# Infini-attention block on one core: q and k projected from raw weights in 32-column tiles, heads regrouped, new orders

## The chip, the cores and the metric

One core of a Trainium2 chip runs the whole program. The metric is the device time of one execution in microseconds (us). The engines are TensorE (PE, with its weight loads shown apart as PEld), VectorE (DVE), ScalarE (ACT), GpSimd (POOL) and SyncE (SP), whose queue issues the transfers between HBM and the on-chip memory and the transposes by DMA.

## The reference

A pre-norm transformer block on one sequence of 2048 tokens, width 640, in bfloat16. Cut to what matters:

```python
x = A_x                                     # (1, 2048, 640)
h = x + A(layernorm(x))                     # attention with memory
h2 = h + silu(layernorm(h) @ w1) @ w2       # F = 1728

def A(x):                                   # H = 32 heads of Dh = 20, N = 4 segments of L = 512
    q, k, v = x @ wq, x @ wk, x @ wv        # split into heads and segments
    for s in range(4):
        p = softmax(qs @ ks.T * Dh**-0.5 + causal_mask)     # within the segment
        a_dot = p @ vs
        a_mem = (phi(qs) @ M) / (phi(qs) @ z + 1e-6)        # phi(t) = t+1 if t>0 else exp(t)
        out[s] = g * a_mem + (1 - g) * a_dot                # g = sigmoid(beta), per head
        M += phi(ks).T @ vs;  z += sum(phi(ks))
    return concat(out) @ wo
```

## The kernel before, in words

**Segments and stages.** The four segments of 512 tokens are worked off in one long list of small tasks. For each segment: layer norm of four blocks of 128 tokens (`n1_st` statistics, `n1_rs` the inverse deviation on POOL, `n1_ap` applied on DVE), a transpose (segment 0: on PE, `n1_tp`, brought back by `n1_te`; later: by DMA, `n1_tr`), the projections of q, k (`pr`, brought from PSUM to SBUF by `qe`) and v (`v`, `ve`), then eight ticks of four heads each. A tick has scores (`qk`), their exponentials on ACT (`e`, line 964 for two heads, 960 for four at once), the causal mask on POOL (`mk`), the product with v (`av`), scaling (`oe`), a transpose back (`td`), from segment 1 on the memory's part (`tm`), normalization (`nm`) and the sum of both (`ad`). `ex`, `pa`, `pb` make phi of k (of q too from segment 1 on); `kt`, `mz`, `ma`, `mb` update the memory. Behind come the output projection (`ot`, `wo`, `rs`), the second layer norm and the two matrix products of the dense part (`h1` with `th` and `s`, `h2` with `o`).

**Names of projection tasks.** `pr021.0` is segment 0, chunk 2 of five, k (0 is q), first three of the five blocks of the contraction; `.1` the other two. A chunk is 128 columns, four heads in four groups of 32 rows, of which a head takes 20. Scores read 20 rows at offsets 0, 32, 64 and 96, each as a tile of its own.

**What stands in the other 12 rows.** Five chunks hold 20 heads in their first 20 rows of each 32. The other 12 heads are packed into the 12 free rows of each 32: the first 12 of a head's 20 dimensions in chunks 0 to 2, the remaining 8 in chunks 3 and 4. Ticks 0 to 4 of a segment read the chunks directly; ticks 5 to 7 read the tile `QKV`, which 12 transfers per segment (`vt`, SP's queue) put together from the chunks. For this packing the columns of wq and wk are copied from the raw weights (in the tile `wraw`, on the place of `sT`) into `wqr` and `wkr` by `re_` tasks on DVE, ACT and POOL (lines 711 and 713) before they are used.

**Order.** Nothing is decided on the chip. A table `ORDER` names every task in the order in which it is emitted, with its engine (`/A`, `/D`, `/G`; `/C` is a PE task done as four tiles of 32 columns, `/W` the exponential of four heads at once) and its buffers. `Tracker` puts in the semaphore waits that the data and buffers need. Each engine works off its own part of the list in order. `fill` tasks are matmuls on zeros at the start.

**PE's three shapes.** A matmul on the whole 128x128 array (line 550), four matmuls of 32 columns side by side (lines 551, 999, 1117), and four matmuls of 20 contraction rows at four row offsets (line 943, the scores).

Of the kernel before, what the change touches and what calls it, by code (L numbers as in the profile page):

```python
# [5 lines left out]
ACT = mybir.ActivationFunctionType  # L6
# [228 lines left out]
class Graph:  # L235
# [52 lines left out]
    def schedule(self):  # L288
# [3 lines left out]
        for row in ORDER:  # L292
# [56 lines left out]
MZB = [0, 2, 4, 6, 9]  # L349
MZN = [2, 2, 2, 3, 3]  # L350

GRP_BLK = [[(0, 0)], [(1, 2)], [(2, 4)], [(3, 6)], [(4, 9)],
           [(0, 1), (3, 7)], [(1, 3), (4, 10)], [(2, 5), (3, 8), (4, 11)]]
# [3 lines left out]
SPLIT0 = ((0, 0), (0, 1))  # L357
# [112 lines left out]
def build(nc, es, A_x, A_wq, A_wk, A_wv, A_wo, A_beta, B_x, B_w1, B_w2, out):  # L470
# [76 lines left out]
    def mms(eng, out, lhsT, rhs, start, stop):  # L547

        if eng != "cols":
            return [lambda e: e.matmul(out, lhsT=lhsT, rhs=rhs, start=start, stop=stop)]  # L550
# [24 lines left out]
    for a in X:  # L575
        a.users += 1
# [329 lines left out]
    def declare_ticks(s):  # L906
# [421 lines left out]
```

## Time and profile before

| what | value |
|---|---|
| runs | 296.78 us median of 3 (296.61 to 297.32) |
| the profiled execution | 297.21 us, its span 295.2 us, clock 1.0 |
| busy: PE, DVE, ACT, POOL | 280.6, 219.0, 216.5, 148.2 us |
| the chain that ended last | PE 64%, ACT 17%, DVE 10%, issue 3% |

The span runs from the first to the last instruction of the profiled execution; 2.0 us of the execution's time lie outside it. The profiled execution is 0.43 us above the median. The chain that ended last is followed back from the last instruction, at each step to what released it; from about 52 us on it is mostly PE, ahead of that mostly ACT.

### The profile page before, as it was taken

What the parts mean: (1) busy time and instruction counts of PE and PEld (TensorE: products, weight loads), DVE (VectorE), ACT (ScalarE), POOL (GpSimd) and SP (SyncE); (2) the same over time, 40 slices, a digit from 0 to 9 for tenths busy, and PEclk for the clock granted to TensorE, in tenths of its full rate; (3) what the DMA queues carried; (4) which work ended last, traced back from release to release, by engine and by line L of the source; (5) the groups of instructions that cost most, each with busy time, mean ns of one, the idle gap of its engine ahead of it and who ended that gap; (6) DMA issues with size and microseconds to landing.
All of it is one profiled execution on the core that took longest, in us unless ns stands there. A gap on an engine that the chain in (4) does not pass through costs nothing.

```text
span 295.2 us, 8471 instructions
## 1 busy us (share of the span) xinstructions
PE 280.6 (95%) x3537; PEld 158.1 (54%) x3561; DVE 219.0 (74%) x447; ACT 216.5 (73%) x263; POOL 148.2 (50%) x297
## 2 busy tenths in 40 slices
PE   7899889899999999999999999999999999999996
PEld 5554434536644545566643564556564657764574
DVE  4788899689999677999879867597655676734614
ACT  5799999799989999957899856979989641004500
POOL 4878777662777436946527552548464621300000
PEclk9999999999999999999999999999999999999999
DMA  7859349476530400442553312303221031330003
GB/s 223 288 151 232 57 115 229 96 235 90 87 66 18 104 4 3 75 100 46 81 135 101 77 27 53 58 2 54 62 69 47 2 67 26 67 91 0 0 2 111
DMA packets 48597, 24.72 MB, mean 84 GB/s; under 512 B 38896, under 2 KB 47472, under 8 KB 48560
## 3 DMA queue, kind: packets, MB, share of 16 engines
q1 hardware_dynamic: 48560, 24.19, 34.9%
q8 instruction: 28, 0.46, 0.6%
q14 instruction: 9, 0.07, 0.1%
HBM read 10.41 MB, written 2.62 MB: 44 GB/s over the span
## 4 chain that ended last, share of the span: by engine, by line
PE 64%; ACT 17%; DVE 10%; issue 3%; DMA 2%; POOL 2%; ACTq 0%; DVEq 0%
PE ps_all L550 47%; ACT PT L964 12%; PE ps_all L551 7%; PE ps_all L943 5%; PE ps_all L999 4%; DVE stt L754 3%; ACT PT L960 2%; DVE xn_rot L772 2%; DVE sT L1222 2%; DMA tT<-otok 2%; ACT th L1216 1%; ACT ex L873 1%; POOL PT L976 1%; DVE x_tok L1181 1%; PE ps_all L1117 1%
## 5 line engine op out<-in xcount | busy, mean ns | idle before, releaser
L964 ACT ACTIVATE PT<-ps_all 128x1024 bf16<-128x1024 f32 x114 | 109.3, 1035 | 15.5 <-PE ps_all L943 14.8
L976 POOL TENSOR_SCALAR_AFFINE_SELECT PT<-PT 128x512 bf16<-128x512 bf16 x128 | 82.0, 649 | 57.5 <-ACT PT L964 32.0
L1216 ACT ACTIVATE th<-ps_all 128x512 f32<-128x512 f32 (+1 forms) x56 | 31.5, 585 | 36.6 <-PE ps_all L550 27.8
L550 PE MATMUL ps_all<-w_sb,sT 128*128 128x320 bf16 x400 | 58.2, 299 | 0.1
L550 PE MATMUL ps_all<-tT,w_sb 128*128 128x512 bf16 x225 | 53.9, 379 | 1.3 <-issue 1.1
L1222 DVE SCALAR_TENSOR_TENSOR sT<-th,ps_all 128x512 bf16<-128x512 f32 (+1 forms) x56 | 36.2, 663 | 17.7 <-ACT th L1216 17.1
L550 PEld LDWEIGHTS ps_all<-w_sb,sT 128*128 128x128 bf16 x400 | 38.1, 98 | 16.6 <-issue 1.5
L960 ACT ACTIVATE PT<-ps_all 128x2048 bf16<-128x2048 f32 x23 | 43.2, 1879 | 3.4 <-PE ps_all L943 3.0
L550 PEld LDWEIGHTS ps_all<-tT,w_sb 128*128 128x128 bf16 x235 | 21.4, 98 | 25.0 <-issue 1.8
L754 DVE BATCH_NORM_STATS2 stt<-x_tok 128x6 f32<-128x320 bf16 x62 | 26.8, 473 | 1.3 <-DMA x_tok<-in_A_x_dram 1.2
L1259 DVE SCALAR_TENSOR_TENSOR x_tok<-ps_all,x_tok 128x640 bf16<-128x640 f32 (+1 forms) x17 | 13.2, 784 | 18.0 <-PE ps_all L550 17.1
L1077 POOL TENSOR_TENSOR otok<-on 128x320 bf16<-128x320 bf16 x24 | 19.2, 806 | 12.5 <-DVE on L1069 12.5
L867 DVE CAST QK<-ps_all 128x512 bf16<-128x512 f32 x26 | 17.9, 687 | 8.0 <-PE ps_all L550 6.5
L764 POOL TENSOR_TENSOR rst<-mvt,eps_c 128x1 f32<-128x1 f32 x32 | 7.0, 219 | 31.9 <-DVE mvt L757 30.0
L550 PE MATMUL ps_all<-tT,wkr 128*128 128x512 bf16 (+1 forms) x87 | 21.7, 368 | 1.0 <-issue 0.5
L772 DVE TENSOR_SCALAR xn_rot<-x_tok,mvt,rst 128x640 bf16<-128x640 bf16 x32 | 17.8, 564 | 4.3 <-POOL rst L766 3.8
L550 PE MATMUL ps_all<-tT,wqr 128*128 128x512 bf16 (+1 forms) x79 | 20.0, 367 | 1.0 <-issue 0.6
L1069 DVE TENSOR_TENSOR on<-ps_all,rd 128x640 bf16<-128x640 f32 x24 | 19.8, 824 | 0.8
L550 PE MATMUL ps_all<-wv_sb,tT 128*128 128x320 bf16 x130 | 19.7, 299 | 0.7 <-issue 0.7
L766 POOL TENSOR_TENSOR rst<-rst,eps_c 128x1 f32<-128x1 f32 x32 | 18.0, 563 | 2.5
L1015 DVE TENSOR_SCALAR oTs<-ps_all,lsc 128x512 bf16<-128x512 f32 x24 | 17.8, 742 | 0.8 <-PE ps_all L999 0.8
L999 PE MATMUL ps_all<-PT,Vx 128*32 128x512 bf16 (+3 forms) x384 | 17.3, 301 | 0.0
(113 smaller groups left out, 379.5 us busy)
## 6 DMA issues: line engine op xcount, KB each, us to landing
out_dram<-x_tok SPq DMA_DIRECT2D x15, 160.0 KB, 1.9
w_sb<-in_B_w_dram SPq DMA_DIRECT2D x5, 432.0 KB, 4.7
x_tok<-in_A_x_dram SPq DMA_DIRECT2D x3, 640.0 KB, 4.3
w_sb<-in_B_w_dram SPq DMA_DIRECT2D x3, 480.0 KB, 4.1
QKV<-QK SPq DMA_DIRECT2D x12, 72.0 KB
wv_sb<-in_A_wv_dram SPq DMA_DIRECT2D x1, 800.0 KB, 8.0
wo_sb<-in_A_wo_dram SPq DMA_DIRECT2D x1, 800.0 KB, 4.9
w_sb<-in_B_w_dram SPq DMA_DIRECT2D x1, 640.0 KB, 5.1
```

Of the source, the lines that this page charges most:

```text
L550: return [lambda e: e.matmul(out, lhsT=lhsT, rhs=rhs, start=start, stop=stop)]
L551: return [lambda e, p=p: e.matmul(out[p:p + 32, :], lhsT=lhsT[:, p:p + 32], rhs=rhs, start=start, stop=stop, tile_position=(0, p)) for p i ...
L754: T.add(DV, lambda e, hh=hh: e.bn_stats(out=stt[:, s, 6 * hh:6 * hh + 6], in_=xb[:, 320 * hh:320 * hh + 320]), reads=R((xa, xsub)), writes ...
L772: T.add(eng, lambda e: e.tensor_scalar(out=xn_rot[:, xn.slot, :], in0=x_tok[:, b % 12, :], scalar1=mvt[:, s, 0:1], scalar2=rst[:, s, :], o ...
L960: T.add(AC, lambda e: e.activation(out=o, in_=src, func=ACT.Exp, scale=SCALE), reads=[("ps", z.slot + q) for z in (a, b) for q in range(2) ...
L964: T.add(AC, lambda e: e.activation(out=pt[:, pta.slot, q0:q0 + 2, 0:width], in_=sc3[:, b0:b0 + 2, 0:width], func=ACT.Exp, scale=SCALE), re ...
L976: fns.append(lambda e, v=v: e.affine_select(out=v, in_=v, pattern=[[0, 4], [1, 128]], compare_op=ALU.is_ge, fill=0.0, base=0, channel_mult ...
L999: fns.append(lambda e, j=j, r=r, h=h, pa=pa, pt=pt, co=co, q0=q0, ji=ji: e.matmul(bank(po)[32 * r:32 * r + 32, q0:hi], lhsT=vtile(vx)[:, j ...
L1069: T.add(DV, lambda e: e.tensor_tensor(out=on[:, ona.slot, :, :].rearrange("p b (x e) -> p b x e", e=DH), in0=v[:, :, :, 0:DH], in1=r2.unsq ...
L1077: T.add(PO, lambda e: e.tensor_tensor(out=o_dst, in0=on[:, ona.slot, 0, :].rearrange("p (i x) -> p i x", i=4), in1=on[:, ona.slot, 1, :].r ...
L1216: T.add(AC, lambda e: e.activation(out=th[:, tha.slot, lo:hi], in_=bank(ps)[:, lo:hi], func=ACT.Tanh, scale=0.5), reads=R((ps, [0])), writ ...
L1222: T.add(DV, lambda e: e.scalar_tensor_tensor(out=sT[:, f, lo:hi], in0=th[:, tha.slot, lo:hi], scalar=1.0, in1=bank(ps)[:, lo:hi], op0=ALU. ...
```

## The change

Tile widths, tables and orders change; the arithmetic stays.

- q and k are projected straight from the raw weights `wq_sb` and `wk_sb`. Chunk c of 0 to 3 takes, for each of four tiles r, the 32 raw columns that start at 160c + 40r: the 20 of head 8c + 2r and the first 12 of head 8c + 2r + 1. Such a product is always four matmuls of 32 columns. Chunk 4 takes the remaining 8 dimensions of the 16 odd heads, for which two tasks (`re_w4q`, `re_w4k`, four copies each, on POOL) fill the tile `w4`. All other `re_` tasks go.
- Ticks 0 to 3 read the chunks directly; ticks 4 to 7 read `QKV`, filled by 8 transfers per segment in place of 12. `HEADS`, `GRP_BLK`, the masks `mm` and `mzc`, the memory's products `mz` and the places in `otok` follow the new grouping (an output tile's four heads lie 40 columns apart).
- wq and wk are loaded in two halves of 320 columns (all five contraction blocks each) in place of a 3 and a 2 block part; the first halves come ahead of segment 1's part of x, the second halves behind it. Loads no longer wait for the `re_` task of `wk`.
- In segment 0 the pieces of a chunk's columns (tokens) are quarters for chunk 0, halves for 1 and 2, wholes for 3 and 4 (`PIECES0`); before, only chunk 0 was in halves. One `qe` task brings back the whole chunk.
- `ORDER` is written anew from end to end. It has no `/W`, 102 `/C` rows in place of 48, and 35 `fill` matmuls in place of 30.

The diff's core:

```diff
-GRP_BLK = [[(0, 0)], [(1, 2)], [(2, 4)], [(3, 6)], [(4, 9)],
-           [(0, 1), (3, 7)], [(1, 3), (4, 10)], [(2, 5), (3, 8), (4, 11)]]
+GRP_BLK = [[(g, 2 * g)] if g < 4 else [(g - 4, 2 * (g - 4) + 1), (4, 4 + g)] for g in range(NG)]
+HEADS = [(8 * (g % 4) + g // 4, 2) for g in range(NG)]
-SPLIT0 = ((0, 0), (0, 1))
+PIECES0 = ([(0, 1), (1, 2), (2, 3), (3, 4)], [(0, 2), (2, 4)], [(0, 2), (2, 4)], [(0, 4)], [(0, 4)])
...
-        if eng != "cols":
+        if eng != "cols" and len(lhsT.shape) == 2:
             return [lambda e: e.matmul(out, lhsT=lhsT, rhs=rhs, start=start, stop=stop)]
-        return [lambda e, p=p: e.matmul(out[p:p + 32, :], lhsT=lhsT[:, p:p + 32], rhs=rhs, start=start, stop=stop,
+        quad = (lambda p: lhsT[:, p // 32]) if len(lhsT.shape) > 2 else (lambda p: lhsT[:, p:p + 32])
+        return [lambda e, p=p: e.matmul(out[p:p + 32, :], lhsT=quad(p), rhs=rhs, start=start, stop=stop,
                                         tile_position=(0, p)) for p in (0, 32, 64, 96)]
+    def chunk(w, kc, c):
+        if c < 4:
+            return (wq_sb, wk_sb)[w][:, kc, 160 * c:160 * c + 160].rearrange("p (r e) -> p r e", e=40)[:, :, 0:32]
+        return w4[:, w, kc, :]
...
-        for z, ks in enumerate(KS):
-            k0_, k1_ = ks[0], ks[-1] + 1
-            load_w(f"{n_}{z}", wraw[:, w_, k0_:k1_, :], cw(src)[:, k0_:k1_, :], -94 + w_, 6.58, [(sT0, [f"{n_}{z}"])], "fix",
-                   (SP,))
+        for z in range(2):
+            load_w(f"{n_}{z}", (wq_sb, wk_sb)[w_][:, :, 320 * z:320 * z + 320], cw(src)[:, :, 320 * z:320 * z + 320],
+                   -94 + w_, 6.58, [(W["w" + n_], [z])], "fix", (SP,))
...
-            virt(3 * r, allq((0, 1, 2)), QKV[p:p + 12, :, :, :], qkt[p + 20:p + 32, 0:3, :, :])
-            virt(3 * r + 1, allq((3, 4)), QKV[p + 12:p + 20, 0:2, :, :], qkt[p + 20:p + 28, 3:5, :, :])
-            virt(3 * r + 2, allq((3, 4)), QKV[p + 12:p + 20, 2, :, :], qkt[p + 28:p + 32, 3:5, :, :])
+            virt(2 * r, allq((0, 1, 2, 3)), QKV[p:p + 12, :, :, :], qkt[p + 20:p + 32, 0:4, :, :])
+            virt(2 * r + 1, allq((4,)), QKV[p + 12:p + 20, :, :, :], qkt[p:p + 32, 4, :, :])
...
-epsc:0 mt0 halfc x0:8 x1:9 x2:0,1 w_q0:0 w_q1 w_k0 w_k1 w_wv:0 n1_st1/A:2,2 ...
+halfc:0 mt0:1 zpad:0 fill1:0 fill1:1 x0:0 fill1:2 fill1:3 vpad2 fill1:4 ...
```

Three places of the order follow. The first is SP's queue at the start of the program, before the change: blocks of x, then all of wq and wk, then wv (line 583 loads x, line 586 the weights).

```order
L583 DMA x_tok<-in_A_x_dram 128x640 x2
L583 DMA x_tok<-in_A_x_dram 128x2x640
L586 DMA sT<-in_A_wq_dram 128x3x640
L586 DMA sT<-in_A_wq_dram 128x2x640
L586 DMA sT<-in_A_wk_dram 128x3x640
L586 DMA sT<-in_A_wk_dram 128x2x640
L586 DMA wv_sb<-in_A_wv_dram 128x5x640
L583 DMA x_tok<-in_A_x_dram 128x4x640
```

The same place after the change (line 595 loads x, 598 weights, 606 beta).

```order
L595 DMA x_tok<-in_A_x_dram 128x640 x2
L606 DMA beta_bc<-in_A_beta_dram 128x32
L595 DMA x_tok<-in_A_x_dram 128x2x640
L598 DMA wq_sb<-in_A_wq_dram 128x5x320
L598 DMA wk_sb<-in_A_wk_dram 128x5x320
L595 DMA x_tok<-in_A_x_dram 128x4x640
L598 DMA w_sb<-in_B_w_dram 64x640
L598 DMA wk_sb<-in_A_wk_dram 128x5x320
L598 DMA wq_sb<-in_A_wq_dram 128x5x320
L598 DMA wv_sb<-in_A_wv_dram 128x5x640
```

beta, the whole of x's segment 1 (128x4x640) and a part of w2 now come ahead of the second halves of wk and wq, and wv is last.

The second place is PE from the first transposes (line 781) to the first scores (line 943), before the change.

```order
L781 MATMUL ps_all<-ident,xn_rot 128x128 x15
L550 MATMUL ps_all<-tT,wqr 128x256 x5
L550 MATMUL ps_all<-tT,wkr 128x256 x6
L550 MATMUL ps_all<-tT,wqr 128x256 x5
L550 MATMUL ps_all<-tT,wkr 128x256 x4
L550 MATMUL ps_all<-tT,wqr 128x512 x3
L943 MATMUL ps_all<-w_sb 128x512 x4
```

The same place after the change (line 782 the transposes, 554 the tiles of 32 columns).

```order
L554 MATMUL ps_all<-tT,wq_sb 32x128 x20
L554 MATMUL ps_all<-tT,wk_sb 32x128 x20
L554 MATMUL ps_all<-tT,wq_sb 32x128 x12
L782 MATMUL ps_all<-ident,xn_rot 128x128 x10
L554 MATMUL ps_all<-tT,wq_sb 32x128 x8
L554 MATMUL ps_all<-tT,wk_sb 32x256 x12
L554 MATMUL ps_all<-tT,wk_sb 32x128 x40
L554 MATMUL ps_all<-tT,wq_sb 32x128 x20
L554 MATMUL ps_all<-tT,wk_sb 32x128 x20
L554 MATMUL ps_all<-tT,wk_sb 32x256 x8
L554 MATMUL ps_all<-tT,wq_sb 32x128 x20
L554 MATMUL ps_all<-tT,wk_sb 32x256 x24
```

The first products now stand ahead of the last two transposes, and the 24 matmuls on the second half of wk (chunk 2) stand right ahead of the first scores, which follow them.

The third place is DVE from the application of segment 0's layer norm to about the scores of tick 1, before the change (line 772 applies the layer norm, 713 copies weights, 867 is `qe`, 754 and 757 statistics).

```order
L772 TENSOR_SCALAR xn_rot<-x_tok,mvt,rst 128x640 x3
L791 CAST tT<-ps_all 128x5x128
L713 COPY wkr<-sT 128x3x4x20
L713 COPY wkr<-sT 128x3x4x12
L713 COPY wkr<-sT 128x2x4x20
L713 COPY wkr<-sT 128x2x4x12
L713 COPY wqr<-sT 128x5x4x20
L713 COPY wqr<-sT 128x5x4x12
L713 COPY wqr<-sT 128x5x4x20
L713 COPY wqr<-sT 128x5x4x12
L867 CAST w_sb<-ps_all 128x256
```

After the change, from the last of the four statistics of segment 1 on (line 868 is `qe`, 834 `ve`, 881 `pa`, 887 `pb`).

```order
L755 BN_STATS stt<-x_tok 128x6 x2
L758 BN_AGGR mvt<-stt 128x2
L773 TENSOR_SCALAR xn_rot<-x_tok,mvt,rst 128x640
L881 TENSOR_SCALAR phiK<-w_sb 128x512
L868 CAST w_sb<-ps_all 128x512
L881 TENSOR_SCALAR phiK<-w_sb 128x512
L773 TENSOR_SCALAR xn_rot<-x_tok,mvt,rst 128x640
L887 TENSOR_TENSOR phiK<-phiK,ex 128x512
L881 TENSOR_SCALAR phiK<-w_sb 128x512
L868 CAST w_sb<-ps_all 128x512
L755 BN_STATS stt<-x_tok 128x6 x2
L758 BN_AGGR mvt<-stt 128x2
```

The weight copies are gone from DVE; the statistics of all four blocks of segment 1 now come ahead of `qe021` (the first of the two rows of line 868) and `qe010` (the second).

402 lines of the change are left out of this document (199 added, 203 removed).

## The prediction

> **What bounds the kernel now.** I read the page first: busy shares and the chain that ended last.
>
> ```profile
> PE 280.6 (95%) x3537; PEld 158.1 (54%) x3561; DVE 219.0 (74%) x447; ACT 216.5 (73%) x263; POOL 148.2 (50%) x297
> PE 64%; ACT 17%; DVE 10%; issue 3%; DMA 2%; POOL 2%; ACTq 0%; DVEq 0%
> ```
>
> PE is busy nearly throughout. The chain in order of time shows where it is not PE that decides:
>
> ```profile
> 14.11 1.88 ACT PT L964 x2
> ...
> 31.52 5.39 ACT PT L964 x6
> ...
> 40.59 7.54 ACT PT L964 x8
> ...
> 48.71 2.86 ACT PT L964 x3
> 51.71 0.40 PE ps_all L943 x4
> ```
>
> From 14.1 to 51.6 us the chain runs along ACT, which makes segment 0's exponentials (line 964); from there on it is mostly PE. Busy time by stage (PE, PEld, DVE, ACT, POOL) agrees:
>
> ```profile
> 10.00:56.60 46.60, 42.40 (x548) 20.94 (x551) 39.79 (x95) 45.20 (x57) 36.17 (x90) 1.00 0.62 155
> 56.60:110.00 53.40, 51.52 (x741) 26.45 (x750) 46.42 (x92) 49.79 (x57) 31.27 (x56) 1.00 0.40 90
> 110.00:230.00 120.00, 117.64 (x1678) 66.48 (x1684) 92.34 (x184) 99.39 (x113) 66.60 (x113) 1.00 0.30 61
> 230.00:295.20 65.20, 62.12 (x537) 39.20 (x533) 34.91 (x63) 15.77 (x28) 8.23 (x16) 1.00 0.16 41
> ```
>
> Up to 56.6 us ACT is busy 97% of the time, PE 91%; then PE 95 to 98%. So there are three questions: when do the first exponentials start, how long does ACT take for segment 0's forty, and does PE need more or less time behind them.
>
> **PE's own work.** Its multiply columns are the same before and after: a product of 128 output columns and the four tiles of 32 that replace it stream the same tokens. What could differ is the cost of a small matmul and of a change between PE's three shapes:
>
> ```profile
> 13.08 0.59 PE L550 MATMUL ps_all<-tT,wqr 128*128 128x512 bf16 x2
> 13.61 0.40 PE L943 MATMUL ps_all<-w_sb 20*128 20x512 bf16 x4
> 13.94 0.61 PE L550 MATMUL ps_all<-tT,wqr 128*128 128x512 bf16 x2
> ...
> 101.76 0.54 PE L1117 MATMUL ps_all<-Vx,phiKt 128*32 128x42 bf16 x48
> 102.12 0.62 PE L551 MATMUL ps_all<-tT,w_sb 128*32 128x512 bf16 x8
> ```
>
> Two matmuls of 512 last 0.59 with an end 0.16 behind the stream, so they stream 0.43 (0.215 each): from 13.08 to 13.51. The scores start at 13.61, 0.10 later; four of them side by side stream 0.21, to 13.82, and the next whole matmul starts at 13.94, 0.12 later. A change of shape costs about 0.11. Counted along PE's list there are 180 changes before and 178 after (many now between scores and 32-column tiles): -0.2 us. The last two rows show 48 matmuls of 32 columns in 0.36 us, 7.5 ns each; four tiles of 128 tokens therefore need no more than their stream of about 0.055 (a quarter of 0.215). [...]
>
> **The start of the program.** These rows carry it:
>
> ```profile
> x_tok<-in_A_x_dram SPq DMA_DIRECT2D x2, 160.0 KB, 2.4
> x_tok<-in_A_x_dram SPq DMA_DIRECT2D x1, 320.0 KB, 3.8
> sT<-in_A_wk_dram SPq DMA_DIRECT2D x1, 320.0 KB, 6.4
> 3.25 1.00 SPq L586 DMA_DIRECT2D sT<-in_A_wk_dram x2
> 11.60 0.51 SPq L594 DMA_DIRECT2D beta_bc<-in_A_beta_dram  x1
> 3.70 0.74 ACT L745 ACTIVATE xn_rot<-x_tok 128x640 bf16<-128x640 bf16 x1 [1.61 <-DMA x_tok<-in_A_x_dram]
> 5.62 1.25 ACT L603 ACTIVATE w_sb<-zpad 128x1280 bf16<-128x1280 bf16 x1
> 9.71 0.82 DVE L791 CAST tT<-ps_all 128x640 bf16<-128x640 f32 x1
> 10.34 0.70 ACT L790 ACTIVATE tT<-ps_all 128x640 bf16<-128x640 f32 x1 [0.60 <-PE ps_all L781]
> 10.44 1.41 DVE L713 COPY wkr<-sT 128x240 bf16<-128x240 bf16 x4
> 14.05 3.89 ACT L964 ACTIVATE PT<-ps_all 128x1024 bf16<-128x1024 f32 x4
> ```
>
> Before, wk's second part is issued at 3.75 and lands 6.4 later, at 10.2; its copy (half of the 1.41) lets k's first product run at 10.44 + 0.71 = 11.15, and the first score exponential starts at 14.05. That removes four copies on this path.
>
> After, the issue of beta (0.51) stands ahead of the third piece of x, which lands at about 1.73 + 0.51 + 3.8 = 6.0 (5.5 before). 2.24 MB had landed by 10.2 with 0.64 of them at 5.5: 0.34 MB per us. wq's first half (0.40 MB) then lands at 7.2, wk's at 8.4, x of segment 1 (0.64) at 10.2, wk's second half (behind 0.08 of w2) at 11.7, wq's at 12.8, wv (0.80) at 15.2. Rows of 640 bytes don't occur among these loads; from "as fast per byte" to "as slow per row as 1280 bytes" (a half 2.4 in place of 1.2) the second half of wk lands between 11.7 and 15.4. I take 11.9, since nothing in the rows makes a row's cost independent of its length.
>
> DVE: the third block's statistics, behind their landing, at 6.1 to 7.3 (1.03, start to start below, and the last one's tail), `n1_ap1` 7.7, `n1_te0` (0.8) 8.55, `n1_ap2` 9.0, `n1_ap3` 9.5, since ACT makes the fourth block's statistics (2.0: from 3.70 to 5.62 and its tail) from 6.0 on. PE: chunk 0's first quarter for q and k at 8.65, the last two transposes at 9.5 to 10.0. ACT brings these back at 9.95 to 10.65 and 10.65 to 11.35 (0.70 each). The last quarters end at 11.7 (k) and 12.2 (q); the 24 matmuls on wk's second half, which the scores now stand behind, need 11.9 and end at 12.85. `qe001`, `qe000` (0.55 each) end at 12.95, the scores come at 13.0, `ex001` ends at 13.5: first exponential 13.55 against 14.05, a gain of 0.5.
>
> **Forty exponentials of segment 0.**
>
> ```profile
> 19.59 0.62 ACT L866 ACTIVATE w_sb<-ps_all 128x512 bf16<-128x512 f32 x1
> 22.01 1.14 ACT L873 ACTIVATE ex<-w_sb 128x512 bf16<-128x512 bf16 x2
> 27.73 20.39 ACT L964 ACTIVATE PT<-ps_all 128x1024 bf16<-128x1024 f32 x22
> 54.70 1.94 ACT L964 ACTIVATE PT<-ps_all 128x1024 bf16<-128x1024 f32 x2 [0.38 <-PE ps_all L943]
> ```
>
> One is 20.39 / 22 = 0.927. Before, the fortieth ends at 54.70 + 1.94 = 56.64: 42.6 from the first, with 2 `qe`, 2 `ve`, 5 `ex` and two small ones between. After, ACT's list has 1 `qe` (0.56), 1 `ve` (0.6) and 4 `ex` (0.55 each) between: 37.1 + 3.4 = 40.5. The rest of that work moves to DVE, so DVE's list must be followed:
>
> ```profile
> 15.19 0.41 DVE L886 TENSOR_TENSOR phiK<-phiK,ex 128x512 bf16<-128x512 bf16 x1
> 15.66 0.69 DVE L867 CAST w_sb<-ps_all 128x512 bf16<-128x512 f32 x1
> 16.27 0.88 DVE L754 BATCH_NORM_STATS2 stt<-x_tok 128x6 f32<-128x320 bf16 x2
> 17.30 0.83 DVE L754 BATCH_NORM_STATS2 stt<-x_tok 128x6 f32<-128x320 bf16 x2
> 42.51 0.28 DVE L880 TENSOR_SCALAR phiK<-w_sb 128x512 bf16<-128x512 bf16 x1
> 48.57 0.82 DVE L833 CAST Vx<-ps_all 128x640 bf16<-128x640 f32 x1
> 50.93 0.44 DVE L772 TENSOR_SCALAR xn_rot<-x_tok,mvt,rst 128x640 bf16<-128x640 bf16 x1
> ```
>
> Start to start: statistics 1.03, `qe` 0.61, `pb` 0.40, `pa` 0.28, `ve` 0.74, `ap` 0.44. From 10.4 (x of segment 1, and a wait's end) to the end of `qe010`: 4 statistics, 2 `ap`, 3 `pa`, 2 `qe`, 1 `pb` and 0.16 = 7.6, so 18.0. The scores of tick 0's last part also read tick 1's q, and start there; ACT would be ready at 18.4, so it waits 0.15. On to `qe041`: 4 statistics, 4 `qe`, 3 `ve`, 4 `ap`, 3 `pb`, 1 `pa` = 12.0, so 30.05; `ex041` is due at 29.5 and waits 0.55. Behind it the next scores wait for `av1`, 0.25. Sum 0.95. The fortieth ends at 13.55 + 40.5 + 0.95 = 55.0, a gain of 1.65.
>
> What is hidden: POOL's eight copies to `w4` (it is busy 36 of 46.6 us; if that cover goes, chunk 4 and with it tick 4 is late), the 1200 more matmuls (same stream), and the other placing in `otok`, on DVE and POOL in the same runs of 20 (POOL is busy 66.6 of the 120 us from 110 on). SP issues 16 fewer `QKV` transfers.
>
> **Behind 55 us** PE has the same work in a new order, 295.2 - 56.6 = 238.6 us of it. By the busy rows, it idles 2 of 53, 2 of 120 and 3 of 65 us there, so an order can win 3 at the most (more only where changes of shape fall away, which they don't), and lose about as much. I take 0.
>
> Sum against the profiled span: 295.2 - 1.65 - 0.2 = 293.35; with the 2.0 outside, 295.35 for such an execution, and 0.43 less for the median: **294.9 us**.
>
> **Rivals.**
> *QKV one tick earlier (slower).* Tick 4 now reads `QKV`; before it was tick 5.
>
> ```profile
> 29.85 6.70 SPq L898 DMA_DIRECT2D QKV<-w_sb  x9
> L943 PEld LDWEIGHTS ps_all<-QKV x48: 90/91/94, 40.0 to 54.3; 20*128 20x128 bf16 x48
> ```
>
> Before, the last copy is issued by 36.55 and first read at 40.0, 3.4 later. After, the copies of chunk 4 follow `qe040` (31.0 by the DVE sum) and SP's queue; at 0.74 each (6.70 / 9) the last is issued from 33.3 on and lands at 35.7 if it takes 2.4, as a small load of x, and at 37.1 if 3.8, as a larger one; I take the first, since a copy moves 0.1 MB or less. Tick 4's scores are due at 36.0. There is no slack: each us by which DVE is later than summed is a us of ACT's waiting. With `qe040` later than 33.8 the whole gain is lost; at 34.7, or with 0.9 lost in each of three segments, it comes out at 297.7 to 299.
> *Short rows load slowly.* wk's second half at 15.4 puts the first exponential at 17.0: +3.5 at the start, part of which DVE's waiting hides: about 297.5.
> *The gain is given back.* Behind 55 us DVE and ACT are busy 87 and 93% up to 110; if ACT's or DVE's waits there decide, PE waits as before at the same places: 296.5.
> *The order gains more.* PE's idle time behind 55 us shrinks by 2: 292.8.
> [...]
>
> **Numbers.** A change within 0.3% (0.9 us) can hardly be told from none. Chances: forecast 0.45 (its own range 293.8 to 296.2; faster 0.40, same 0.05), order gains more 0.13, gain given back 0.13 (same 0.11), QKV late or new waits of that kind 0.19, short rows 0.07 (same 0.02), starts 25 ns apart 0.03 (same). Faster 0.55, same 0.21, slower 0.24. The range 292.2 to 298.6 leaves out a tenth on each side.
>
> **What would show it.** First exponential (line 964) near 13.5 and the fortieth near 55; PE's first scores behind the rows on wk's second half; no wait of PE or ACT on `QKV` at 36; changes of shape still 0.1. The prediction is wrong if wk lands after 13, if ACT waits more than 2 us in all between 14 and 55, or if PE's idle time behind 60 us grows by more than 2.

## The result, and the profile after

The changed kernel takes **312.57 us** (median of 4 runs, 311.87 to 313.69) against 296.87 us (296.61 to 297.32) for the kernel before: ratio **1.053 [1.050, 1.057]**. It is 15.7 us slower; 294.9 was forecast, with a range up to 298.6. The profiled execution took 311.87 us, its span is 310.1 us. Times are medians; two disturbed executions, one of e10 (308.6 us) and one of e12 (1569), and the stages of these two runs are left out.

The page of the kernel after: busy time, the chain that ended last, and the queue that brings instructions (packets, MB, share of 16 engines' span).

```profile
PE 286.1 (92%) x4750; PEld 163.4 (53%) x4764; DVE 219.0 (71%) x442; ACT 216.0 (70%) x279; POOL 147.5 (48%) x287
PE 62%; DVE 12%; DMA 9%; ACT 7%; issue 4%; SPq 3%; POOL 2%; DVEq 0%; ACTq 0%
q8 instruction: 37, 0.61, 0.8%
```

The work of each engine is the old one, but it stands in a longer span. In the chain DMA has grown to 9% (2% before), issue to 4% (3%), and 3% of SP's queue are new; ACT has fallen from 17% to 7%. To find the place, both executions are cut at the same events: the first score exponential, and the ends of the 40th (segment 0), the 80th, 120th and 160th. First after (stretch, its length, then the busy times of PE, PEld, DVE, ACT, POOL, the granted clock, the transfers' busy share, GB/s):

```profile
0.00:18.30 18.30, 12.87 (x267) 9.39 (x271) 10.22 (x32) 10.43 (x20) 15.16 (x58) 0.92 0.91 280
18.30:66.10 47.80, 41.77 (x775) 21.05 (x772) 33.70 (x70) 41.04 (x46) 26.67 (x53) 0.92 0.89 155
66.10:123.20 57.10, 52.47 (x1132) 27.54 (x1136) 49.23 (x100) 51.80 (x68) 31.76 (x51) 1.00 0.39 55
123.20:185.10 61.90, 59.26 (x1041) 33.52 (x1038) 50.94 (x102) 51.01 (x67) 34.79 (x60) 1.00 0.42 71
```

and the same stretches of the kernel before:

```profile
0.00:14.10 14.10, 10.62 (x77) 7.35 (x79) 8.99 (x26) 9.48 (x20) 9.62 (x36) 1.00 0.77 251
14.10:56.60 42.50, 38.72 (x517) 18.57 (x519) 36.30 (x84) 42.03 (x50) 32.47 (x79) 1.00 0.61 149
56.60:110.70 54.10, 52.22 (x753) 26.80 (x762) 46.94 (x93) 50.47 (x57) 31.27 (x56) 1.00 0.40 89
110.70:170.60 59.90, 58.08 (x971) 33.09 (x968) 51.18 (x105) 51.10 (x59) 35.81 (x62) 1.00 0.38 76
```

So 4.2 us are lost ahead of the first exponential, 5.3 in segment 0's forty, 3.0 and 2.0 in the next two stages, and 0.4 behind (the last two stages take 60.8 and 64.2 us, before 60.8 and 63.8). There are three losses to explain.

**Loss 1, the start.** PE's rows at the place where the prediction had the last quarters and the first scores (start, length, in brackets the idle time ahead and its cause):

```profile
11.74 0.67 PE L554 MATMUL ps_all<-tT,wk_sb 128*32 128x128 bf16 x28
12.24 0.28 PE L554 MATMUL ps_all<-tT,wq_sb 128*32 128x128 bf16 x8
15.92 0.51 PE L554 MATMUL ps_all<-tT,wq_sb 128*32 128x128 bf16 x12 [3.40 <-issue]
...
17.64 0.61 PE L943 MATMUL ps_all<-w_sb 20*128 20x512 bf16 x4
...
22.14 1.06 PE L554 MATMUL ps_all<-tT,wq_sb 128*32 128x256 bf16 x32 [0.81 <-issue]
```

Up to 12.24 all is as forecast. Then PE stops for 3.4 us in the middle of one task of 20 matmuls, where no wait stands in the program, and once more, for 0.8, at 21.3. "Issue" means that it waited for nothing that the profile shows. 37 packets of q8 for 4750 + 4764 matmuls and weight loads are one for 257 instructions; before, the page had this row:

```profile
q8 instruction: 28, 0.46, 0.6%
```

that is 254 for a packet. So PE's instructions come in blocks of about 256, as transfers, which the page counts on the 16 engines that carry the data too (0.8% of their span beside 42.7% for q1). Counted from zero along all of PE's records (matmuls, weight loads and semaphore instructions), number 448 is the last ahead of the 3.4 us, and number 704, one block further, the last ahead of the 0.8. Numbers 192 to 448 took 3.1 us (9.2 to 12.3); the block's packet begins 4.0 us behind number 192, at 13.3, and ends at 14.4, ahead of 15.92. From number 2240 to 7360 the packets begin within 1.3 us of every 256th number behind 192. In the kernel before, number 192 comes at 16.3 and the packet begins at 16.2; number 448 comes only at 31.8.

**Loss 2, tick 3 of segment 0.** Ticks 0 to 2 have 6, 4 and 6 exponentials, and the gap comes behind the 16th. ACT's rows around it (the first exponential, the last two of tick 2, the first two of tick 3), then PE's wait and its first scores from `QKV` (tick 4), DVE's wait, and SP's queue.

```profile
18.31 1.02 ACT L964 ACTIVATE PT<-ps_all 128x1024 bf16<-128x1024 f32 x1 [0.71 <-PE ps_all L943]
...
36.90 1.94 ACT L964 ACTIVATE PT<-ps_all 128x1024 bf16<-128x1024 f32 x2
43.22 1.94 ACT L964 ACTIVATE PT<-ps_all 128x1024 bf16<-128x1024 f32 x2 [4.38 <-PE ps_all L943]
```

```profile
40.82 0.46 PE L552 MATMUL ps_all<-ident,oTs 128*128 128x84 bf16 x4 [3.48 <-DVE oTs L1015]
...
46.77 0.40 PE L943 MATMUL ps_all<-QKV 20*128 20x512 bf16 x4 [0.27 <-ACT PT L964]
```

```profile
39.21 0.29 DVE L881 TENSOR_SCALAR phiK<-w_sb 128x512 bf16<-128x512 bf16 x1 [3.28 <-DMA phiKt<-phiK]
```

```profile
33.27 0.90 SPq L899 DMA_DIRECT2D QKV<-w_sb  x1
34.22 1.22 SPq L1107 DMA_TRANSPOSE phiKt<-phiK  x1
35.48 7.54 SPq L899 DMA_DIRECT2D QKV<-w_sb  x7
```

The transpose `kt02`, issued at 34.2 between the `QKV` copies, lands at 39.1. `pa041` on DVE waits for it, and behind `pa041` stand `qe040`, `oe1` and `oe0`, on which PE and the last four copies wait. PE's own wait is for `oe1` (`oTs`), ahead of tick 3's scores, which read a chunk directly; tick 4's scores then wait for no copy.

**Loss 3, behind the fortieth exponential.** PE's waits there, of which the kernel before had only 0.2 us, of the first kind (total, times, longest):

```profile
PE ps_all L552 <- DMA tT<-otok: 2.6, 2, 1.6
PE ps_all L552 <- DMA sT<-otok: 1.5, 2, 1.1
PE ps_all L943 <- DMA QKV<-QK: 1.2, 1, 1.2
```

### The profile page after: what moved, and what is told of

It reads as the page before. It is cut to its first block, busy times and chain, and to the rows that moved or that the text cites. A ratio compares the mean times of both kernels' runs of the same rounds, so it can differ in the third digit from the quotient of the medians.

```text
span 310.1 us, 10883 instructions
## 1 busy us (share of the span) xinstructions
PE 286.1 (92%) x4750; PEld 163.4 (53%) x4764; DVE 219.0 (71%) x442; ACT 216.0 (70%) x279; POOL 147.5 (48%) x287
## 3 DMA queue, kind: packets, MB, share of 16 engines
q1 hardware_dynamic: 50032, 24.84, 42.7%
## 4 chain that ended last, share of the span: by engine, by line
PE 62%; DVE 12%; DMA 9%; ACT 7%; issue 4%; SPq 3%; POOL 2%; DVEq 0%; ACTq 0%
PE ps_all L552 33%; PE ps_all L554 18%; ACT PT L964 7%; PE ps_all L943 5%; PE ps_all L999 4%; DMA tT<-otok 3%; SPq L1165 2%; DMA phiKt<-phiK 2%; DVE QK L868 1%; DMA QKV<-QK 1%; DVE oTs L1015 1%; DMA x_tok<-in_A_x_dram 1%; DMA sT<-otok 1%; SPq L899 1%; DVE phiK L887 1%
## 5 line engine op out<-in xcount | busy, mean ns | idle before, releaser
L964 ACT ACTIVATE PT<-ps_all 128x1024 bf16<-128x1024 f32 x160 | 154.8, 1027 | 33.6 <-PE ps_all L943 32.3
L1221 DVE SCALAR_TENSOR_TENSOR sT<-th,ps_all 128x512 bf16<-128x512 f32 (+1 forms) x56 | 36.2, 662 | 14.3 <-ACT th L1215 13.8
L552 PE MATMUL ps_all<-tT,w_sb 128*128 128x512 bf16 x144 | 34.0, 379 | 1.3 <-issue 0.5
L1258 DVE SCALAR_TENSOR_TENSOR x_tok<-ps_all,x_tok 128x640 bf16<-128x640 f32 (+1 forms) x17 | 13.2, 781 | 25.8 <-PE ps_all L552 25.7
L1078 POOL TENSOR_TENSOR otok<-on 128x320 bf16<-128x320 bf16 x24 | 19.4, 810 | 17.8 <-DVE on L1070 15.8
L554 PE MATMUL ps_all<-tT,w_sb 128*32 128x512 bf16 x420 | 26.2, 380 | 0.1
L554 PE MATMUL ps_all<-tT,wq_sb 128*32 128x512 bf16 (+2 forms) x420 | 21.8, 332 | 4.8 <-issue 4.2
L552 PEld LDWEIGHTS ps_all<-tT,w_sb 128*128 128x128 bf16 x155 | 14.3, 98 | 16.7 <-issue 0.9
L1015 DVE TENSOR_SCALAR oTs<-ps_all,lsc 128x512 bf16<-128x512 f32 x28 | 20.7, 744 | 3.4 <-PE ps_all L999 3.3
L554 PE MATMUL ps_all<-tT,wk_sb 128*32 128x512 bf16 (+2 forms) x420 | 21.9, 342 | 0.0
L943 PE MATMUL ps_all<-QKV 20*128 20x512 bf16 (+3 forms) x256 | 15.9, 300 | 3.7 <-DMA QKV<-QK 1.2
L552 PE MATMUL ps_all<-wo_sb,tT 128*128 128x320 bf16 x110 | 16.6, 299 | 2.6 <-DMA tT<-otok 2.6
L1180 DVE TENSOR_TENSOR x_tok<-ps_all,x_tok 128x640 bf16<-128x640 f32 x16 | 13.0, 815 | 6.9 <-PE ps_all L552 5.5
```

The source lines that it names most:

```text
L554: return [lambda e, p=p: e.matmul(out[p:p + 32, :], lhsT=quad(p), rhs=rhs, start=start, stop=stop, tile_position=(0, p)) for p in (0, 32, ...
L943: fns.append(lambda e, j=j, o=o, r=r, q0=q0, q1=q1, qa=qa, ka=ka: e.matmul(ps_all[:, o:o + q1 - q0], lhsT=ka[32 * r:32 * r + DH, 128 * j:1 ...
L964: T.add(AC, lambda e: e.activation(out=pt[:, pta.slot, q0:q0 + 2, 0:width], in_=sc3[:, b0:b0 + 2, 0:width], func=ACT.Exp, scale=SCALE), re ...
L1015: f = lambda e: e.tensor_scalar(out=o, in0=i_, scalar1=lsc[:, g:g + 1], scalar2=None, op0=ALU.mult)
L1078: T.add(PO, lambda e: e.tensor_tensor(out=o_dst, in0=on[:, ona.slot, 0, :].rearrange("p (i r e) -> p i r e", i=4, r=4), in1=on[:, ona.slot ...
L1221: T.add(DV, lambda e: e.scalar_tensor_tensor(out=sT[:, f, lo:hi], in0=th[:, tha.slot, lo:hi], scalar=1.0, in1=bank(ps)[:, lo:hi], op0=ALU. ...
```

## The experiments

The kernel before has 296.7 to 297.1 us in each group of runs. The stages in the profiled executions of the kernels that are compared below (first exponential's start, then the ends of exponentials, us); one execution can lie some us from the median, e1's by 2.5:

| kernel | first | 40th | 80th | 120th | 160th | span |
|---|---|---|---|---|---|---|
| before | 14.1 | 56.6 | 110.7 | 170.6 | 231.4 | 295.2 |
| after | 18.3 | 66.1 | 123.2 | 185.1 | 245.9 | 310.1 |
| e1, whole products in segment 0 | 13.9 | 61.1 | 118.3 | 181.0 | 240.3 | 305.0 |
| e5, e1 and late bulk loads | 13.5 | 58.0 | 115.2 | 179.3 | 238.6 | 304.4 |
| e6, e5 and `kt02` early, `pa041` late | 13.7 | 58.0 | 115.1 | 177.9 | 238.4 | 303.8 |
| e8, after without 24 copies | 17.8 | 65.9 | 121.6 | 182.5 | 241.6 | 305.8 |
| e13, tiles kept, start mended | 14.7 | 59.5 | 116.8 | 177.6 | 236.8 | 301.1 |

**e1: fewer instructions at the start.**

```diff
+        if c < 4 and s == 0:
+            return (wq_sb, wk_sb)[w][:, kc, 160 * c:160 * c + 128]
```

> The changed kernel, with segment 0's products of chunks 0 to 3 done as one matmul on the whole array instead of four tiles of 32 columns; for that they take 128 adjacent weight columns, so q and k of segment 0 are other numbers. 270 matmuls and as many weight loads fewer on PE, the same columns streamed, the same loads, the same order. Theory (PE runs dry: the refill of its instructions waits behind the loads while PE uses up 256 instructions in 3 us): the 3.4 us of issue at 12.5 and the 0.8 at 21.3 go, first exponential 13.5 to 14.2 in place of 18.3, time 306 to 309.5. Rival 1 (column tiles of 128 tokens or the late weights hold the start, not the instructions): first exponential still after 16. Rival 2 (the start is made good or lost again by DVE's wait at 36 to 43): first exponential early, time 311 to 313.

309.14 us (306.68 to 309.37). q and k of segment 0 are other numbers in it. PE's rows, and ACT's first exponential and the gap at tick 3:

```profile
12.34 0.44 PE L552 MATMUL ps_all<-tT,wq_sb 128*128 128x128 bf16 x5
12.62 0.82 PE L552 MATMUL ps_all<-tT,wk_sb 128*128 128x256 bf16 x6
13.47 0.39 PE L945 MATMUL ps_all<-w_sb 20*128 20x512 bf16 x4
```

```profile
13.92 1.02 ACT L966 ACTIVATE PT<-ps_all 128x1024 bf16<-128x1024 f32 x1
...
38.73 22.41 ACT L966 ACTIVATE PT<-ps_all 128x1024 bf16<-128x1024 f32 x24 [4.07 <-PE ps_all L945]
```

The issue wait is gone; the last quarter and the products on wk's second half follow without a pause, and the first exponential is 4.4 us earlier. The fortieth is 5.0 earlier, the span 5.1; by the medians the gain is 3.4. So the tiles caused loss 1, and not the loads alone; that it is their number, and not their shape, e13 shows, which keeps them. Loss 2 stays.

**e2 and e11: loads moved back, the same instructions.** e2 moves x of segment 2 and wv behind the first transpose of segment 1 and three parts of w2 behind the last; e11 leaves wv where it was.

```diff
-... w_w2_5 ... w_k1 ... w_q1 ... w_wv:0 w_w2_4 x8:8,9,10,11 ... w_w2_3 ... n1_tr6:1 ... n1_tr4 ...
+... w_k1 ... w_q1 ... n1_tr6:1 x8:8,9,10,11 w_wv:0 ... n1_tr4 w_w2_4 w_w2_5 w_w2_3 ...
```

> The changed kernel with the same instructions; on SP's queue the loads of wv, of x for segment 2 and of three parts of w2 are moved behind the transposes of segment 1 (x and wv behind the first of them, w2 behind the last). Theory (the refill waits behind data on the transfer engines): with less data under way at 9 to 13 us the refill comes within 2 us of its due time at 9.25, PE's issue wait at 12.5 falls from 3.4 to under 1 us, first exponential 13.5 to 15, time 306 to 310. Rival (so many instructions per us can't be supplied at all, whatever the loads): the wait stays at 2.5 us or more and the time within 2 of 312.6.

> The changed kernel, all products as tiles of 32 columns, with x for segment 2 moved behind the first transpose of segment 1 and three parts of w2 behind the last; wv stays where it is. Theory (the refill waits behind whatever is under way at 9 to 14 us; wv, x of segment 1 and the second halves of wk and wq still are): PE's issue wait at 12.5 lies between the 3.4 of the changed kernel and the 1.7 that it had with wv moved too, first exponential 16 to 17.5, no wait for wv, time 309.5 to 312. Rival (those 1.4 MB don't matter): 18.3 and 312.6 again.

e2: 315.63 us (314.96 to 316.83), e11: 313.06 (312.61 to 314.02). The issue wait of e2 and its wait for wv, then the issue wait of e11:

```profile
14.10 0.35 PE L554 MATMUL ps_all<-tT,wq_sb 128*32 128x128 bf16 x12 [1.68 <-issue]
...
24.79 1.53 PE L554 MATMUL ps_all<-wv_sb,tT 128*32 128x320 bf16 x20 [5.52 <-DMA wv_sb<-in_A_wv_dram]
```

```profile
15.58 0.51 PE L554 MATMUL ps_all<-tT,wq_sb 128*32 128x128 bf16 x12 [3.16 <-issue]
```

At the same instruction PE waits half as long when wv is not under way (first exponential 15.6), so the loads are the other half of the cause. Neither range of e2's expectation was met: its time was spoiled by wv itself, which then came 5.5 us too late. In e11 the rival was right: what is issued from 8.3 us on, shortly ahead of the block's due time of 9.2 and behind it (and a small part of w2 at 4.3), delays it by 0.2 us only. wv, issued at 7.2, is the load that counts.

**e3 and e4: DVE's wait taken out of the way.**

```diff
-... qe041/D:0 pa041:1 mk1a ... qe040/D ... oe1/D:1 av0:6 oe0/D:0 td1:3 ...
+... qe041/D:0 mk1a ... qe040/D ... oe1/D:1 av0:6 oe0/D:0 pa041:1 td1:3 ...
```

> The changed kernel with one DVE task moved: pa041 (phi of k for chunk 4, which needs the buffer that the transpose kt02 frees) stands behind qe040, oe1 and oe0 instead of ahead of them. Theory (DVE's 3.3 us of waiting for the slow transpose at 36 holds back qe040, oe1, oe0 and so PE and ACT): the wait still stands in DVE's rows but nothing queues behind it that PE needs, ACT's wait of 4.4 us at 38.8 falls under 1.5, the fortieth exponential ends near 63 instead of 66, time 308.5 to 310.5. Rival (the QKV copies, which land late, hold tick 4 by themselves): the wait moves to tick 4's scores, time 311.5 to 313.

> Both moves together: the loads behind the transposes and pa041 behind oe0. If the two losses are separate, their gains add: fortieth exponential near 58 to 60, time 303 to 307. If they share one slack (QKV's copies or DVE in order), the time is within 1.5 of the better of the two alone. The rest up to 296.9 is then what is lost behind the fortieth exponential (about 5.4).

e3: 312.14 us (311.80 to 315.74), e4 (with e2's loads): 316.13 (314.80 to 317.18), outside both of its readings; PE waits 5.5 us for wv in it as in e2. In e3 the rival held. DVE's wait is still there, now behind the work that PE needs, and PE waits for a transpose of segment 1's x ahead of tick 3 and for the copies ahead of tick 4 instead (PE's rows in e3, in the execution of 315.74 us):

```profile
40.11 1.51 PE L552 MATMUL ps_all<-wv_sb,tT 128*128 128x320 bf16 x5 [1.82 <-DMA tT<-xn_rot]
...
48.31 0.62 PE L943 MATMUL ps_all<-QKV 20*128 20x512 bf16 x4 [3.37 <-DMA QKV<-w_sb]
```

ACT still waits 2.9 and 3.0 us ahead of these two ticks. So DVE's 3.3 us only covered waits on other transfers; their lengths are those of one execution, 3.6 us above the median.

**e5 and e6: the bulk loads out of the copies' way.** On top of e1, wo, w1 and two parts of w2 (4.1 MB) go behind the last transpose of segment 2's x; e6 also sends `kt02` ahead of the first copy and `pa041` behind `oe0`.

```diff
-... w_w1_1:0 w_w1_4 ... w_w1_3 ... w_w1_0 w_w1_2 ... w_wo:0 ... vt00:0 ... kt02:1 vt02 ... w_w2_0 w_w2_1 ... n1_tr9 ...
+... vt00:0 ... kt02:1 vt02 ... n1_tr9 w_wo:0 w_w1_0:0 w_w1_1 w_w1_2 w_w1_3 w_w1_4 w_w2_0 w_w2_1 ...
```

> The kernel with segment 0's products as whole matmuls (first exponential 13.9, 309.1 us median, 306.7 when profiled), with one thing more: the loads of wo, all of w1 and two parts of w2 (4.1 MB) are moved on SP's queue behind the last transpose of segment 2's x, so that nothing is loaded between 17 and 50 us but the transposes and the QKV copies. Theory (bulk loads slow the transpose kt02, 4.8 us in place of 2.7, and the copies, 1.0 us for a packet of 8 KB, and these hold back tick 4 of segment 0): the 24 copies of 8 KB take under 0.6 us each, kt02 lands in under 3 us, ACT's 4.1 us of waiting at 34.7 falls under 2, time 303 to 306. Rival (the copies are slow by themselves, since all eight now come only behind the last products of q and k, in few long packets): ACT still waits 3 us or more, time 307.5 to 310.

> The same, and besides kt02 ahead of the first QKV copy on SP's queue and pa041 behind oe0 on DVE. If DVE's wait for kt02 is then what is left of the gap at tick 4: ACT's wait there under 1 us, time 1 to 3 us below the kernel before it. If the copies decide: the wait moves to tick 4's scores (PE waits for QKV), same time within 1 us.

e5: 306.40 us (305.51 to 308.43), e6: 305.69 (305.26 to 306.36). ACT's rows of e5 at ticks 3 and 4, and the DVE row that waited before:

```profile
35.27 3.77 ACT L966 ACTIVATE PT<-ps_all 128x1024 bf16<-128x1024 f32 x4 [0.52 <-PE ps_all L945]
39.45 18.56 ACT L966 ACTIVATE PT<-ps_all 128x1024 bf16<-128x1024 f32 x20 [0.41 <-PE ps_all L945]
```

```profile
32.28 0.29 DVE L883 TENSOR_SCALAR phiK<-w_sb 128x512 bf16<-128x512 bf16 x1
```

The gap is gone, so loss 2 was contention: loads, transposes and copies on the same engines (their busy share at 30 to 40 us is 1.23 in the kernel after, counting overlaps, 0.60 in e5 and 0.39 before). `kt02` lands 3.1 us behind its issue, 4.9 in the kernel after, and that time holds no waiting in SP's queue. The packets of 8 KB were no faster, though (median 1.07 us, 1.04 in the kernel after), against the expectation. And of the 3.1 us won at the fortieth exponential, the span kept 0.6 (the medians 2.7): loss 3 grew.

```profile
PE ps_all L552 <- DMA tT<-otok: 3.6, 2, 2.2
```

e6's further moves brought 0.7, inside the spread.

**e7: tiles of 32 columns in the kernel before.**

```diff
-... pr000x.0:0 pr000x.1 qe000x:0 pr001x.0:2 ...
+... pr000x.0/C:0 pr000x.1/C qe000x:0 pr001x.0/C:2 ...
```

> The kernel before with all products of q and k of segment 0 as four tiles of 32 columns, as its order can mark them: 210 matmuls and as many weight loads more on PE, nothing else changed. Theory (it is the late refill, not the tiles): PE reaches the 192nd instruction at about 12.5, where its transfers are half as busy as after the change, the refill comes 1 to 2 us later, before the 448th at about 15.5: no issue wait over 1 us, time 296 to 298.5. Rival (tiles of 32 columns cost by themselves, or a refill is always too slow for them): issue waits of 2 us or more ahead of the first exponentials, time 299 or more.

299.19 us (298.32 to 302.66), ratio 1.010 [1.004, 1.017]: the time is in the rival's range, the place of the wait is not the rival's. The start is untouched: first exponential 13.9, no issue wait in segment 0, number 192 at 11.6 and 448 only at 17.7; the fortieth exponential is 0.6 later. But there is an issue wait at another place, 160 us on:

```profile
172.77 1.26 PE L550 MATMUL ps_all<-tT,w_sb 128*32 128x512 bf16 x18 [1.49 <-issue]
```

The last instruction ahead of it is number 5056, right behind 80 small memory products that ran in 0.84 us; numbers 4800 to 5056 took 3.5 us. In e5, number 2496 is the last ahead of an issue wait of 0.90 at 82.3. 448, 2496 and 5056 lie 8 and 10 times 256 apart. The instructions added at the start (204 matmuls and 180 weight loads by the records, 210 of each expected) had moved the borders of the blocks. That one of them now fell into a run of short tiles fits the wait; it was not tried alone.

**e8: without the copies of segments 1 to 3.** The tasks `vt1*`, `vt2*`, `vt3*` issue nothing.

```diff
+            if name[:2] == "vt" and name[2] != "0":
+                return
```

> The changed kernel without the 24 QKV copies of segments 1 to 3 (it leaves them out: ticks 4 to 7 of these segments read segment 0's QKV again); the start and segment 0 stay as they are. It sizes what is lost behind the fortieth exponential (244.0 us there against 238.6 before). Theory (the copies' long packets delay the transposes of otok and the scores of ticks 4): PE's waits for transposes of otok and for QKV, 5.3 us, fall under 2.5, time 307.5 to 310. Rival (the transposes come late because of the order, not of the copies): 311.5 to 313.

307.63 us (307.34 to 311.74), 4.9 less than the changed kernel. Behind the fortieth exponential 239.9 us are left, where the changed kernel takes 244.0 and the kernel before 238.6. PE's waits:

```profile
PE ps_all L552 <- DMA sT<-otok: 0.7, 1, 0.7
PE ps_all L552 <- DMA tT<-otok: 0.6, 1, 0.6
```

So the 24 copies cost the changed kernel 4.1 us there, of a loss of 5.4. The kernel before pays for copies of its own, and no run says how much: the 4.1 are the copies' whole price, and the part that the change added stays open.

**e9 and e10: the copies smaller and earlier, or otok's transposes ahead of them** (both on e6).

```diff
-            virt(2 * r, allq((0, 1, 2, 3)), QKV[p:p + 12, :, :, :], qkt[p + 20:p + 32, 0:4, :, :])
+            for u in range(2):
+                virt(3 * r + u, allq((2 * u, 2 * u + 1)), QKV[p:p + 12, 2 * u:2 * u + 2, :, :],
+                     qkt[p + 20:p + 32, 2 * u:2 * u + 2, :, :])
```

```diff
-... ot0:0 ot1 ... vt14:0 ... ot2 vt10 ... ot3 ...
+... ot0:0 ot1 ... ot2 ... ot3 vt14:0 vt10 ...
```

> The kernel with whole products in segment 0, late bulk loads, kt02 early and pa041 late (305.7 us, fortieth exponential at 58.0), with the QKV copies made smaller and earlier: a copy of four chunks (12 packets of 8 KB) becomes two of two chunks (4 KB), and in every segment the four copies of chunks 0 and 1 go out as soon as these are there and QKV is free (in segment 0 ahead of the last transpose of x, in segments 1 and 2 ahead of the transposes of otok). The bytes are the same. Theory (the copies come late and long, behind the last products, and delay the scores of ticks 4 and the transposes of otok): PE's waits for QKV, 2.3 us, go, those for transposes of otok fall from 5.5 to about 3, time 301.5 to 304. Rival (the bytes count, not when and how they are sent): 305 to 307.

> The kernel of 305.7 us with only this changed: in segments 1 and 2 the QKV copies that stood between the four transposes of otok on SP's queue (two and four of them) stand behind them. Theory (a transpose waits for the copy ahead of it): PE's waits for transposes of otok fall from 5.5 to about 2.5, at the price of up to 1 us more for QKV, time 302.5 to 304.5. Rival (the transposes are late by their own 4 us when four go out together): within 1 us of 305.7.

e9: 308.82 us (308.23 to 310.57), worse than both theories had it, though PE's waits for otok's transposes fell from 5.5 to 3.2. One new wait of PE, and one that was 1.3 in e6:

```profile
PE ps_all L554 <- DMA tT<-xn_rot: 2.8, 1, 2.8
PE ps_all L947 <- DMA QKV<-w_sb: 2.8, 1, 2.8
```

Twelve copies need 9.2 us of SP's queue in place of 7.4; the early ones stand ahead of the last transpose of x, and the last copy is issued 2 us later than in e6. So the place in the queue counts; what the smaller packets did by themselves this run can't tell, since both were changed. e10: 303.44 us (302.73 to 305.41), 2.2 less than e6.

**e12: e10 without the copies of segments 1 to 3.**

> The kernel with whole products in segment 0, late bulk loads, kt02 early, pa041 late and otok's transposes ahead of the copies (304.4 us), without the 24 QKV copies of segments 1 to 3 (left out: ticks 4 to 7 there read segment 0's QKV again). Theory (the copies cost about 4 us behind the fortieth exponential wherever they stand): 299.5 to 301.5. Rival (what they cost was mostly the transposes between them, which now stand ahead): 302.5 to 304.5.

302.66 us (301.90 to 302.81). The rival held: with otok's transposes ahead, the copies cost 0.8 us more and not 4.

**e13: the tiles kept, the start mended.** Chunk 0 in halves, x of segment 2 behind the first transpose, w1, wo and w2 late, and e6's and e10's moves.

```diff
-PIECES0 = ([(0, 1), (1, 2), (2, 3), (3, 4)], ...
+PIECES0 = ([(0, 2), (2, 4)], ...
```

> The changed kernel with all products as tiles of 32 columns from the right columns, but chunk 0 in two halves instead of four quarters (80 matmuls and 80 weight loads fewer ahead of the first scores), x of segment 2, w2, wo and w1 loaded late as before, kt02 early, pa041 late, otok's transposes ahead of the copies. Theory (instructions per us against a late refill): PE reaches its 448th instruction some 2 us later, the issue wait is under 1.5 us instead of 3.4, first exponential 14.3 to 16, time 304 to 307.5. Rival (tiles themselves hold the start): first exponential after 17, time over 308.

303.74 us (302.82 to 306.14), with e14 the best of the versions that compute all of the change. PE's first scores and the product of v that waits later; DVE's row that it waits for:

```profile
14.26 0.39 PE L942 MATMUL ps_all<-w_sb 20*128 20x512 bf16 x4
...
23.21 0.85 PE L551 MATMUL ps_all<-wv_sb,tT 128*128 128x320 bf16 x5 [2.05 <-DVE w_sb L867]
```

```profile
21.46 0.89 DVE L754 BATCH_NORM_STATS2 stt<-x_tok 128x6 f32<-128x320 bf16 x2 [2.22 <-DMA x_tok<-in_A_x_dram]
```

No issue wait is left at the start: PE passes number 192 at 10.7 and number 448 only at 15.6, behind the block's packet (13.2 to 14.3). Tiles do not hold the start; too many of them in too little time do (numbers 192 to 448 took 4.9 us here, 3.1 in the kernel after). The wait at 21 is the price of the later load of x.

**e14 and e15: this wait taken out, and then the copies.** e14 moves the statistics of segment 2's first block behind `ve00`; e15 also leaves out the 24 copies.

> The mended kernel with tiles (303.7 us) with the statistics of segment 2's first block moved behind the copy of v's first block on DVE. Its load lands at about 21.3, and in the kernel before DVE waits 2.2 us for it with the copy of q behind it, which PE's first product of v waits for (2.05). Theory: that wait falls to under 0.7 us, the fortieth exponential ends 1 to 2 us earlier than 59.5, time 301.5 to 303. Rival (what is won there is lost again before the end, as when the loads were moved): 303 to 304.5.

> The same without the 24 QKV copies of segments 1 to 3 (left out: ticks 4 to 7 there read segment 0's QKV again). With otok's transposes already ahead of the copies: if the copies are the rest of the loss behind the fortieth exponential (3 us), the stage from the fortieth to the eightieth takes 54.5 to 55.5 us and the time is 298.5 to 300.5. If the rest is the order of PE's and DVE's work (DVE has 49 us of work in that stage where it had 47), the stage stays at 56 or more and the time at 300.5 to 302.5.

e14: 304.06 us (301.55 to 304.51). DVE's wait is gone, PE's wait there is 0.6, ACT has no wait of 2.2 at tick 1, yet the fortieth exponential ends at 60.4 (59.5 in e13): the rival held. A part of this may be the clock: it was granted at 0.51 from 40.5 to 44.0 us, and at 1.00 in e13. e15: 301.12 us (300.75 to 304.25), 2.9 less than e14 but in the rival's range: the copies are a part of the rest, not all of it. How large a part stays open, since e12 has 0.8 for the same copies, and e14's and e15's times spread over 3.0 and 3.5. The stage that the expectation names took 59.6 us in e15's profiled execution, which at 304.25 us was 3.1 above the median, and decides nothing. No version beats the kernel before.

## Why the prediction was wrong, point by point

- **The step that failed first**: under "what is hidden", "the 1200 more matmuls (same stream)". The stream is the same, and sets of four tiles of 128 tokens start 58 ns apart (five in 0.29 us, 8.61 to 8.90), as the sum had it (0.055). No run shows the starts 25 ns apart for which a chance of 0.03 stands: in these sets a tile starts every 14.5 ns on average, and the 48 small matmuls of before every 7.5 ns. But a tile costs two instructions whatever it streams (4750 matmuls and 4764 weight loads by the records), and their supply was not costed. The page of before had the row (28 packets of q8), its 254 instructions to a packet, and transfers busy eight tenths at the start (0.80 up to 10 us). It cost 4.4 us ahead of the first exponential: 18.3, and 13.9 without it in e1 (forecast 13.55). The waits at such borders came to 3.4, 1.5, 0.9 and 0.8 us.
- **Loads**: right. wk's second half, issued at 5.7, landed at 12.1 (forecast 11.9); short rows were no rival. Only wv came late, at 16.7 for 15.2.
- **QKV one tick earlier**: a rival with 0.19. Its direction was right, its mechanism only in part, and its price of 0.9 us a segment too small. `qe040` came at 40 (33.8 was the point of no gain) and ACT lost 4.4 us, but ahead of tick 3, which doesn't read `QKV`: DVE's wait for `kt02` held back `oe1`. Tick 4, late by then, waited for no copy. What the rival names shows where DVE's wait is out of the way: PE then waits for the copies ahead of tick 4, 1.0 us in e5 and 3.4 in e3. The term that failed there is the copies' time to land, taken as a small load's 2.4 us: the last one, issued at 35.4 in e5 and 41.5 in e3, was there only at 39.0 and 48.3, 3.6 and 6.8 later. In the segments behind, PE waited 1.2 us for copies and 4.1 for the transposes between them, which its chance covers only as "new waits of that kind".
- **"SP issues 16 fewer QKV transfers"**: counted as hidden, and as a count true. That two of them, and later four, stand between otok's transposes in the new order was not followed, although SP's queue was named.
- **DVE's sum** had `qe040` end at 31.0 without any wait for a transpose. `pa041` takes the buffer that `kt02` frees; in e5, where DVE doesn't wait for `kt02`, `qe040` ends at 33.2, so the sum itself was 2 us short.
- **Behind 55 us "I take 0"**: it was 5.4. That an order could "lose about as much" as 3 us looked at PE's idle time alone; transfers were not followed.
- **Changes of shape** still cost about 0.1 us each: two sets of four scores of 256 tokens, 0.21 of streaming, start at 36.29 and the next shape at 36.62. Right, and without weight.

Open: in e13, 5.9 us remain. e14 shows that its wait at 21 us is not what they hang on, and leaving out the copies won 2.9 in e15 and 0.8 in e12. The stage from the 40th to the 80th exponential takes 57.3 us there (54.1 before), with 49.1 us of DVE's work in it (46.9) and PE's waits scattered over DVE's results, 0.2 to 1.1 each. That this is DVE's order is argued, not shown.

## What to carry to other kernels

Replacing one matmul by four tiles keeps the stream and quadruples the instructions: divide them by the blocks on the instruction queue's row (one for 257 here), and ask how long a block takes to come while loads run (about 5 us here, from number 192 to the end of the packet). A copy on the queue of a transpose was paid by PE, which waited for the transpose (2.2 us, e10), so count each transfer at its place in the queue and not by its bytes. A wait taken off one engine won little where another lay under it: DVE's 3.3 us in e3 won 0.4 by the medians, its 2.2 us in e14 nothing.

## What was not expected of the hardware

- PE ran dry at numbers 448, 704 (the kernel after), 2496 (e5) and 5056 (e7), with waits of 3.4, 0.8, 0.9 and 1.5 us. All four lie whole blocks of 256 behind number 192, near which the first packet begins in the kernel before (16.2 us, and 16.3): that a block is asked for there, one block ahead of its use, is inferred, not shown. At 448 it was 3.4 with wv under way and 1.7 without (e2).
- PE paid twice for its long waits. After the 3.4 us the granted clock fell:

```profile
10.00:20.00 10.00, 6.53 (x217) 4.97 (x221) 4.98 (x18) 4.67 (x8) 7.65 (x26) 0.83 1.18 310
```

The first scores took 0.61 us at 17.64, against 0.39 in e1. After the 3.5 us ahead of tick 3 it was 0.69 from 40 to 50 us, and in e1, behind a wait of 3.1, 0.83 from 30 to 40. In the kernel after it was 0.50 from 15.5 to 18.9 us. The length of the wait alone does not tell: 0.51 followed one of 1.65 us in e15 (70.3 to 73.8 us) and one of 1.49 in e14 (40.5 to 44.0); over either execution the mean was 0.994. Behind 1.49 in e7 the clock stayed at 1.00 (160 to 180 us), and so it did in e13, with 2.05 us the longest.
- In the kernel after, copies between rows of the on-chip memory in packets of 8 KB took 1.0 us each among other transfers (the median of 192), and 2048-byte ones (512 packets) mostly 0.08 to 0.30.
